# Moving one half of k^T v across the partitions by transfers on GpSimd's queue instead of matmuls and copies, for four of eight batches

## The chip, the cores and the metric

The kernel runs on one core of one Trainium2 chip. Its time is the time on the device in microseconds (us). Beside the time of a run, the profile gives a span, which is the time from the first to the last instruction of one profiled execution.

## The reference

Two blocks follow each other. The first is a linear attention without a softmax over 8 batches, 8 heads, 576 rows and 64 columns a head, with a norm of each row:

```python
kv = np.einsum('bhsd,bhse->bhde', k, v)
out = np.einsum('bhsd,bhde->bhse', q, kv)
rms = np.sqrt(np.mean(out * out, axis=-1, keepdims=True) + 1e-06)
return (out / rms * g_norm)
```

Its result, as 4608 tokens of 512 columns, enters a mixture of 8 experts: a token with `x @ w_skip > 0` goes to the expert with the largest of `x @ w_gate`, whose two layers (512 to 1024, relu, 1024 to 512) are weighted by the softmax and added to the token; the others stay as they are. All is in fp32.

## The kernel before, in words

**Stages.** The attention stage comes first. The experts follow, each with its weights loaded, its tokens gathered by indirect transfers, two layers, and the results scattered. Order on every engine is written out by hand (`tc.manual_schedule()`): what a function emits first runs first on its engine, and each engine and each DMA queue takes its instructions in that order.

**Units.** The attention's products with q are cut into 36 units. Batches 0 to 3 are units 0 to 15, four each; units 16 and 17 take the ninth row of each group of nine for these four batches together; batches 4 to 7 are units 18 to 33, and units 34 and 35 are again the ninth rows. The loop `for n in range(NU + 2)` emits a unit a turn: `turn(n + 1)` transposes q on PE (L460) and copies it on ACT (L463), `root(n - 1)` takes a root on ACT (L525), then come the jobs listed as "early", `values(n)` (PE L496, or L504 for the ninth rows, then ACT's squares L510), `squares` (DVE L518) and `norm(n - 1)` (DVE L532 and L537), then the jobs listed as "pe". In the batch's first two units `values` also transposes the ninth row (`turn_8`, PE L479 and ACT L482). `finish` and `scale` give GpSimd its work: small sums for the logits (L554, L558, L562), the product with g_norm (L567), and now and then a store of 256 KB on its own queue (L598). The other stores and all loads are on SP's queue.

**k^T v.** For each batch `state` builds k^T v in PSUM with 72 small matmuls (L379, 64x64 tiles of the array, shown as 144 instructions), cut into portions of so many of the 18 row groups, one portion a unit; `portions` gives for each batch the first unit and the sizes. After the last portion ACT copies the sums to `kvd` (L386), two diagonal blocks, called `own(b, w)`: w = 0 lies in partitions 0 to 63, w = 1 in 64 to 127. `state_t` (PE L393, ACT L396) turns them, `state_m` (PE L402, ACT L405) multiplies them with the gate's weights and adds 9 columns at each end.

**The exchange.** `values` needs each block in both halves of the partitions. `state_s` does this with two matmuls against an identity (PE L411, 64 partitions, 292 columns) into the other half of PSUM and two copies on ACT (L415) into `kvds[b % KVD]`. It is listed one unit after `state_m`. The first `values` that reads batch b's block is its first unit (18, 22, 26 and 30 for batches 4 to 7).

**What hangs on the units.** Streams of routing work (`choose`, `rank`, `number`, `rank_experts`, `early`) begin after units 12 and 22 and emit two or four DVE instructions a unit. At unit 30 `early` places PE's L869 after `values(30)`; its result gives the rows of the first gather (L863, on GpSimd's queue), whose tokens PE turns in L801. The first expert's first layer (L814) follows the attention stage.

Of the kernel before, what the change touches and what calls it, by code (L numbers as in the profile page):

```python
# [17 lines left out]
def kernel(  # L18
# [43 lines left out]
    nc = tc.nc  # L62
# [18 lines left out]
    KVD = 5  # L81
# [46 lines left out]
    def load_kv(b):  # L128
        if b < B:
            for name, to in (("k", kts), ("v", vts)):  # L130
                to[b] = kv_pool.tile([P, 4, C, D], FP32, tag=name, name=name)
            for u in range(2):
                for src, t in ((k, kts[b]), (v, vts[b])):
                    load_part(t, src, b, u)

    def load_q(b):
        if b < B:
            qts[b] = load(q_pool, "q", q, b)
# [65 lines left out]
    kvds = []  # L204
# [89 lines left out]
    for lo, m, _ in runs:  # L294
# [26 lines left out]
        out=srow[:, :].rearrange("p (r c) -> p r c", c=CK),  # L321
# [33 lines left out]
    def own(b, w):  # L355

        return kvds[b % KVD][w * 64:(w + 1) * 64, :, w, w, :]
# [13 lines left out]
    def state(b, some):  # L371

        kt, vt = kts[b], vts[b]
        for i in some:
            u, c = divmod(i, C)
            for w in range(2):
                for a in range(2):
                    r = slice(a * 64, (a + 1) * 64)
                    nc.tensor.matmul(  # L379
                        out=sum_ps[w * 64:(w + 1) * 64, a, u, :],  # L380
                        lhsT=kt[r, 2 * u + w, c, :], rhs=vt[r, 2 * u + w, c, :],
                        start=(c == 0), stop=(c == C - 1), skip_group_check=True)
        if some.stop < 2 * C:
            return
        for w in range(2):
            nc.scalar.copy(out=own(b, w)[:, :, G:G + 2 * D].rearrange("p u (a d) -> p a u d", a=2),  # L386
                           in_=sum_ps[w * 64:(w + 1) * 64, :, :, :])

    def state_t(b):
        for u in range(2):  # L390
            for w in range(2):
                r = slice(w * 64, (w + 1) * 64)
                nc.tensor.matmul(out=kvT_ps[:, u, r], lhsT=kvds[b % KVD][:, u, w, w, G:G + 2 * D],  # L393
                                 rhs=ident[:, r], start=True, stop=True)
        kvT = att_pool.tile([P, 2, P], FP32, tag="kvT", name="kvT", bufs=1)
        nc.scalar.copy(out=kvT[:, :, :], in_=kvT_ps)  # L396
        kvTs[b] = kvT

    def state_m(b):
        kvT = kvTs.pop(b)  # L400
        for u in range(2):
            nc.tensor.matmul(out=lg_ps[:, u, :, :, :], lhsT=kvT[:, u, :], rhs=gw_b[:, u, :, :, :],  # L402
                             start=True, stop=True)
        for w in range(2):
            nc.scalar.copy(out=ends_of(own(b, w)), in_=lg_ps[w * 64:(w + 1) * 64, :, :, w, :])  # L405

    def state_s(b):

        for w in range(2):
            r, o = slice(w * 64, (w + 1) * 64), slice((1 - w) * 64, (2 - w) * 64)  # L410
            nc.tensor.matmul(out=sw_ps[o, :], lhsT=ident[r, r], rhs=own(b, w), start=True, stop=True,  # L411
                             skip_group_check=True)
        for w in range(2):
            o = slice((1 - w) * 64, (2 - w) * 64)
            nc.scalar.copy(out=kvds[b % KVD][o, :, w, 1 - w, :],  # L415
                           in_=sw_ps[o, :].rearrange("p (u k) -> p u k", u=2))


    units = []
    nq = 0  # L420
# [21 lines left out]
    def at(step, part, job):  # L442
        todo.setdefault((step, part), []).append(job)
# [448 lines left out]
    for b in range(KNOWN // S // 4 * 4, KNOWN // S):  # L892
        nc.gpsimd.dma_start(
            out=out[b * S:(b + 1) * S, :].rearrange("(p c) d -> p c d", c=C)[:, C - 1, :],
            in_=zero)

    starts = {}
    for n, (_, b, i, _) in enumerate(units):
        if i is not None:
# [8 lines left out]
    turn(1)  # L908
    state_s(0)

    portions = {1: (1, (10, 8)), 2: (4, (6, 6, 6)), 3: (7, (5, 6, 7)), 4: (11, (3, 4, 4, 4, 3)),
                5: (16, (3, 2, 6, 7)), 6: (20, (4, 4, 5, 5)), 7: (24, (4, 4, 5, 5))}
    over = 0
    for b, n in starts.items():
        if b:
            step, counts = portions[b]
            i = 0
            for count in counts:
                at(step, "pe", lambda b=b, some=range(i, i + count): state(b, some))
                i += count  # L920
                step += 1
            assert i == 2 * C and step < n and step - len(counts) > over - 1
            at(step, "early", lambda b=b: state_t(b))
            at(step, "pe", lambda b=b: state_m(b))
            at(step + 1, "early" if step + 1 == n else "pe", lambda b=b: state_s(b))
            over = step
        at(over, "end", lambda b=b: load_kv(b + 3))

        at(n + 2, "end", lambda b=b: load_q(b + 2))
# [61 lines left out]
    with tc.tile_pool(name="wpool_b", bufs=1, reuse_waits="tile") as wpool_b, \  # L991
# [524 lines left out]
        with tc.If(n_rounds > 1):  # L1516
            with tc.For_i(1, n_rounds, 1):
# [8 lines left out]
                    out=left[:, :].rearrange("p (r c) -> p r c", c=CK),  # L1526
# [39 lines left out]
```

## Time and profile before

| What | Value |
|---|---|
| Time, median of 3 runs | 377.03 us (375.7 to 379.55) |
| The profiled execution's own time | 378.6 us |
| Its span | 376.7 us |
| Mean granted TensorE clock | 0.992 |
| PE busy | 362.9 us, 96% of the span |
| PE weight loads busy | 314.8 us, 84% |
| DVE, ACT, GpSimd busy | 244.3, 142.9, 122.7 us |
| Data moved | 81.70 MB, mean 217 GB/s |
| PE L411, one instruction | 405 ns, 32 of them |
| ACT L415, one copy | 397 ns, 16 of them |

A row of a timeline gives the start, the time to the end of the last instruction, the engine, the line, the operation with the tile written and the tiles read, and how many instructions it merges; in brackets, how long the engine sat idle before and what ended that. PE's rows overlap, because matmuls are pipelined: the time that a row holds PE is read from its start to the start of the next. DMA share is the mean busy share of the core's 16 DMA engines.

### The profile page before, as it was taken

The numbers are of one execution on the slowest core, as the hardware profiler recorded it, in microseconds if no ns is written. First come the engines' busy times: TensorE is split into PE (matmuls) and PEld (weight loads), VectorE is DVE, ScalarE is ACT, GpSimd is POOL, SyncE is SP. The second block draws the span as 40 slices with busy tenths as digits, with TensorE's granted clock in tenths as the row PEclk, the third lists the DMA queues.
The fourth block names the chain that finished last, engine by engine and source line by source line (L and its number), as shares of the span: only waits on it lengthen the run. The fifth ranks groups of instructions, "written<-read, shape, count | busy, mean of one in ns | idle before, by whom it ended". The sixth has DMA issues, their size and how long they took to land.

```text
span 376.7 us, 9624 instructions
## 1 busy us (share of the span) xinstructions
PE 362.9 (96%) x3848; PEld 314.8 (84%) x3848; DVE 244.3 (65%) x626; ACT 142.9 (38%) x383; POOL 122.7 (33%) x195
## 2 busy tenths in 40 slices
PE   8899999999988999999999999999999999999994
PEld 4687897898977948779979987988998998998983
DVE  3355367767787763566766675876876776878831
ACT  2466576666773212214402430430440430431420
POOL 7035467655668435323013302202302302102003
PEclk9999999999998999999999999999999999999998
DMA  8999999996487718967427362671762762700001
GB/s 289 395 391 391 401 405 396 405 384 206 132 302 213 232 39 281 392 237 252 168 98 222 114 225 76 239 244 46 284 197 72 274 209 80 269 3 28 30 1 53
DMA packets 32039, 81.70 MB, mean 217 GB/s; under 512 B 2474, under 2 KB 2482, under 8 KB 31988
## 3 DMA queue, kind: packets, MB, share of 16 engines
q1 hardware_dynamic: 28176, 69.47, 52.0%
q0 software_dynamic: 3792, 11.53, 9.2%
q8 instruction: 32, 0.52, 0.6%
q14 instruction: 19, 0.16, 0.1%
q10 hardware_dynamic: 20, 0.02, 0.0%
HBM read 66.80 MB, written 14.48 MB: 216 GB/s over the span
## 4 chain that ended last, share of the span: by engine, by line
PE 82%; issue 6%; DMA 3%; ACT 3%; DVE 3%; POOL 2%; SPq 0%; POOLq 0%; DVEq 0%; ACTq 0%
PE bank L1192 44%; PE bank L1124 9%; PE o_ps L496 6%; PE sum_ps L379 4%; PE bank L1112 4%; PE q_ps L460 3%; PE g_ps L393 2%; DMA v<-in_v_dram 2%; PE bank L1093 2%; PE q_ps L814 1%; DMA xg<-out_dram,src 1%; DVE rs L518 1%; DVE xl L537 1%; ACT sq L510 1%; PE g_ps L411 1%
## 5 line engine op out<-in xcount | busy, mean ns | idle before, releaser
L1202 ACT COPY p<-bank 128x128 f32<-128x128 f32 (+6 forms) x70 | 20.8, 297 | 99.2 <-PE bank L1192 88.5
L1192 PE MATMUL bank<-xt,w 128*128 128x128 f32 (+5 forms) x336 | 55.4, 288 | 0.0
L567 POOL TENSOR_TENSOR xb<-xl,g_b 128x512 f32<-128x512 f32 x36 | 43.5, 1211 | 32.5 <-DVE rs L532 30.6
L1323 POOL DMA_INDIRECT out_dram<-xg,rows x14 | 14.4, 1027 | 120.8 <-DVE xg L1320 117.6
L1192 PEld LDWEIGHTS bank<-xt,w 128*128 128x128 f32 x336 | 47.0, 190 | 1.9 <-DVE bank L1196 1.4
L1196 DVE TENSOR_TENSOR bank<-bank,p 128x128 f32<-128x128 f32 (+6 forms) x70 | 23.6, 337 | 30.2 <-PE bank L1192 29.1
L496 PE MATMUL o_ps<-kvd,qT 128*128 128x146 f32 x240 | 35.8, 290 | 1.0 <-ACT kvd L415 0.7
L1192 PE MATMUL bank<-xs,s 128*128 128x128 f32 (+5 forms) x224 | 36.7, 289 | 0.0
L518 DVE TENSOR_REDUCE rs<-sq 128x8 f32<-128x512 f32 x36 | 24.6, 682 | 15.3 <-ACT sq L510 15.1
L496 PEld LDWEIGHTS o_ps<-kvd,qT 128*128 128x128 f32 x240 | 31.6, 188 | 2.0 <-ACT kvd L415 1.5
L1124 PE MATMUL bank<-w,ht 128*32 128x128 f32 (+2 forms) x436 | 33.2, 318 | 0.0
L1192 PEld LDWEIGHTS bank<-xs,s 128*128 128x128 f32 x224 | 31.1, 190 | 1.0 <-ACT p L1202 0.8
L537 DVE TENSOR_TENSOR xl<-o_ps,rs 128x584 f32<-128x584 f32 x34 | 26.1, 767 | 4.5 <-DVE rs L532 0.5
L1124 PEld LDWEIGHTS bank<-w,ht 128*32 128x32 f32 (+2 forms) x436 | 19.3, 120 | 11.6 <-issue 8.3
L1192 PE MATMUL bank<-t,ht 128*128 128x256 f32 x112 | 27.0, 384 | 0.0
L1192 PE MATMUL bank<-w,ht 128*128 128x256 f32 x112 | 26.5, 380 | 0.0
L510 ACT ACTIVATE sq<-o_ps 128x512 f32<-128x512 f32 x34 | 20.3, 597 | 15.0 <-PE o_ps L496 14.4
L379 PE MATMUL sum_ps<-v,k 64*64 64x64 f32 x1152 | 24.7, 223 | 0.8 <-issue 0.6
L1192 PE MATMUL bank<-t,hs 128*128 128x256 f32 x112 | 25.3, 379 | 0.0
L379 PEld LDWEIGHTS sum_ps<-v,k 64*64 64x64 f32 x1152 | 20.9, 134 | 4.7 <-issue 1.7
L1084 POOL DMA_INDIRECT xg<-out_dram,src x14 | 13.8, 985 | 33.3 <-DMA out_dram<-xg,rows 17.3
L1192 PEld LDWEIGHTS bank<-t,ht 128*128 128x128 f32 x112 | 20.8, 190 | 3.9 <-issue 1.2
(217 smaller groups left out, 671.0 us busy)
## 6 DMA issues: line engine op xcount, KB each, us to landing
w<-in_moe_w_dram SPq DMA_DIRECT2D x16, 2048.0 KB, 10.0
k<-in_k_dram SPq DMA_DIRECT2D x16, 576.0 KB, 9.1
v<-in_v_dram SPq DMA_DIRECT2D x16, 576.0 KB, 11.0
q<-in_q_dram SPq DMA_DIRECT2D x16, 576.0 KB, 10.5
out_dram<-xb SPq DMA_DIRECT2D x29, 256.0 KB, 8.0
out_dram<-xb POOLq DMA_DIRECT2D x7, 256.0 KB, 6.4
xg<-out_dram,src POOLq DMA_INDIRECT x16, 3.5
out_dram<-xg,rows POOLq DMA_INDIRECT x16, 6.0
```

What stands on the lines that cost most here:

```text
L379: nc.tensor.matmul(out=sum_ps[w * 64:(w + 1) * 64, a, u, :], lhsT=kt[r, 2 * u + w, c, :], rhs=vt[r, 2 * u + w, c, :], start=(c == 0), stop ...
L496: nc.tensor.matmul(out=ps[:, w, 0:2 * PK].rearrange("p (r k) -> p r k", r=2)[:, :, cols], lhsT=qT[:, w, a, :], rhs=kvds[b % KVD][:, u, w, ...
L510: nc.scalar.activation(out=sq[:, :, :, :], in_=heads(ps, G, G + 2 * D), func=ACT.Square)
L518: nc.vector.tensor_reduce(out=rs[:, :, :], in_=sq[:, :, :, :].rearrange("p x y (a d) -> p x (y a) d", a=2), axis=AX.X, op=ALU.add)
L537: nc.vector.tensor_tensor(out=xl[:, :, :, :].rearrange("p x y (a k) -> p x (y a) k", a=2), in0=ps[:, :, 0:2 * PK].rearrange("p x (h k) -> ...
L567: late.append((lambda: nc.gpsimd.tensor_tensor(out=xb[:, :, 4 * u * D:(4 * u + 4) * D].rearrange("p r (w x) -> p r w x", w=2), in0=xl[:, : ...
L1112: nc.tensor.matmul(out=hps[:, cols], lhsT=w_sb[r][0][:, dc, f * P:(f + 1) * P], rhs=xt[:, dc, cols], start=(dc == 0), stop=(dc == DC - 1))
L1124: nc.tensor.matmul(out=yps[q * m:(q + 1) * m, 0:n], lhsT=ht(f)[:, off:off + m], rhs=w_sb[r][1][:, f, q * n:(q + 1) * n], start=(f == 0), s ...
L1192: nc.tensor.matmul(out=out, lhsT=lhsT(i), rhs=rhs(i), start=start and i == 0, stop=i == k - 1, skip_group_check=True)
L1196: nc.vector.tensor_tensor(out=to, in0=x, in1=y, op=ALU.add)
L1202: nc.scalar.copy(out=t, in_=x)
L1323: ins = nc.gpsimd.indirect_dma_start(out=cut_rows(m)[:, :], out_offset=bass.IndirectOffsetOnAxis(ap=rows[:, col:col + 1], axis=0), in_=x, ...
```

## The change

For batches 4 to 7 `state_x` takes the place of `state_s`. It issues two transfers on GpSimd's queue, from each diagonal block to the other half of the partitions in the same tile. They are listed in the same unit as `state_t` and `state_m`, behind `state_m`. The portions of these four batches become one fewer and larger, so that `state_t`, `state_m` and the transfers come one unit earlier (units 15, 19, 23 and 27, where before `state_t` stood in 16, 20, 24 and 28 and `state_s` in 17, 21, 25 and 29). Batches 0 to 3 stay as they are. The lines of the new kernel behind this point are 6 to 9 higher.

```diff
+    def state_x(b):
+
+        for w in range(2):
+            o = slice((1 - w) * 64, (2 - w) * 64)
+            nc.gpsimd.dma_start(out=kvds[b % KVD][o, :, w, 1 - w, :], in_=own(b, w))
...
-    portions = {1: (1, (10, 8)), 2: (4, (6, 6, 6)), 3: (7, (5, 6, 7)), 4: (11, (3, 4, 4, 4, 3)),
-                5: (16, (3, 2, 6, 7)), 6: (20, (4, 4, 5, 5)), 7: (24, (4, 4, 5, 5))}
+    portions = {1: (1, (10, 8)), 2: (4, (6, 6, 6)), 3: (7, (5, 6, 7)), 4: (11, (4, 5, 5, 4)),
+                5: (16, (5, 6, 7)), 6: (20, (6, 6, 6)), 7: (24, (6, 6, 6))}
...
-            at(step + 1, "early" if step + 1 == n else "pe", lambda b=b: state_s(b))
+            if b < 4:
+                at(step + 1, "early" if step + 1 == n else "pe", lambda b=b: state_s(b))
+            else:
+                at(step, "pe", lambda b=b: state_x(b))
```

## The prediction

> **What bounds the kernel now.** I read the page's chain that ended last first, then the chain in order of time over the attention stage, then the timelines of PE and of GpSimd there, then the busy time by stretches with the DMA share, and last the line that already sends plain transfers from GpSimd's queue.
>
> The page says which engine sets the end:
>
> ```profile
> PE 82%; issue 6%; DMA 3%; ACT 3%; DVE 3%; POOL 2%; SPq 0%; POOLq 0%; DVEq 0%; ACTq 0%
> PE bank L1192 44%; PE bank L1124 9%; PE o_ps L496 6%; PE sum_ps L379 4%; PE bank L1112 4%; PE q_ps L460 3%; PE g_ps L393 2%; DMA v<-in_v_dram 2%; PE bank L1093 2%; PE q_ps L814 1%; DMA xg<-out_dram,src 1%; DVE rs L518 1%; DVE xl L537 1%; ACT sq L510 1%; PE g_ps L411 1%
> ```
>
> PE carries it, and L411, the swap that the change removes, is 1% of the span. The change touches only the stage before about 107 us, so I ask what ends that stage. PE's timeline near its end (start us, us, engine, line, operation):
>
> ```profile
> 100.73 1.22 PE L496 MATMUL o_ps<-kvd,qT 128*128 128x146 f32 x8
> 101.78 0.53 PE L402 MATMUL g_ps<-gw_b,kvT 128*128 128x36 f32 x4
> 102.15 0.64 PE L460 MATMUL q_ps<-ident,q 128*128 128x128 f32 x4
> 102.62 1.17 PE L496 MATMUL o_ps<-kvd,qT 128*128 128x146 f32 x8
> 103.71 0.71 PE L411 MATMUL g_ps<-kvd,ident 64*64 64x292 f32 x4
> ...
> 105.06 1.18 PE L496 MATMUL sum_ps<-kvd,qT 128*128 128x146 f32 x8
> 106.29 0.69 PE L869 MATMUL g_ps<-bv,oha_k 128*128 128x4 bf16 x22
> ...
> 111.94 0.63 PE L801 MATMUL q_ps<-ident,xg 128*128 128x128 f32 x4 [1.10 <-DMA xg<-out_dram,src]
> ```
>
> Each L496 row is one unit's `values`; 100.73, 102.62 and 105.06 are units 28, 29 and 30, and unit 30 is the first that reads batch 7's swapped half. L869 stands behind it on PE, its rows start the gather that L801 waits 1.10 us for, and all to 117 us hangs on that. So what counts is when unit 30's product and L869 run: lateness there passes to the end one to one.
>
> GpSimd's timeline where it sends half a block of rows as a plain transfer, and the answer on that line:
>
> ```profile
> 99.74 0.58 POOL L598 DMA_DIRECT2D out_dram<-xb  x1 [0.29 <-POOL xb L567]
> ```
>
> ```profile
> DMA to landing us min/median/max: 4.5/6.4/7.4
> ```
>
> And the stretches (length, busy us of PE, PEld, DVE, ACT, POOL, then PEclk, DMA share, GB/s):
>
> ```profile
> 70.00:80.00 10.00, 10.00 (x195) 9.22 (x194) 7.58 (x18) 6.61 (x19) 6.25 (x13) 1.00 1.04 402
> 80.00:90.00 10.00, 9.79 (x175) 8.66 (x177) 6.86 (x17) 7.19 (x18) 6.54 (x11) 1.00 0.71 235
> 90.00:98.00 8.00, 7.96 (x160) 7.29 (x161) 6.19 (x22) 5.16 (x14) 3.90 (x9) 1.00 0.45 167
> 98.00:106.00 8.00, 8.00 (x97) 6.91 (x96) 6.74 (x18) 6.16 (x16) 5.44 (x9) 1.00 0.83 264
> ...
> 112.00:118.00 6.00, 4.19 (x83) 3.50 (x84) 4.70 (x10) 3.21 (x8) 5.44 (x11) 1.00 0.60 146
> 118.00:122.00 4.00, 4.00 (x16) 4.00 (x16) 2.95 (x7) 0.49 (x2) 3.33 (x9) 0.57 0.95 285
> ```
>
> PE has no free time from 70 to 106 us, so instructions taken off it there are worth their time. But the DMA engines are full to about 85 us and again at 98 to 106, and a plain transfer of GpSimd's needs 4.5 to 7.4 us there. The last two rows show the clock: after a stretch with PE 70% busy it fell to 0.57.
>
> **What the Trainium skill says.** "DMA: Bandwidth & Descriptors", "Anatomy of one DMA — SWDGE (gpsimd) path", prices a transfer at 2.0 us plus its bytes over 436e3 per us: for one half of the exchange (64 x 2 x 146 x 4 = 74,752 bytes) an estimate of 2.2 us. The trace differs: 256 KB stores would take 2.6, and took 6.4. Its "Queues, rings and completion order" says that an engine takes turns between queues a packet at a time; in the trace's packet records the stores' first packet starts 3.9 to 4.4 us after the issue in all six stores before 100 us, and 2.4 us in the one of 113.93, where less was in flight. So sharing delays the start more than the data. "TensorEngine Tiling (Array Packing)", "Key Properties", says that a change of tiling mode drains TensorE. The trace agrees in size: L379 rows of 32, 40, 48 and 56 instructions hold PE for 0.63, 0.74, 0.86 and 0.97 us to the next row, so 0.0143 each and 0.17 fixed. "TensorE: Matmul & The Clock Gate", "What's actually happening", has the clock fall to half after a slack window of 3.4 us; here it was at half from 118.2 to 121.6 us.
>
> **The change part by part.** Removed from PE: the swap for batches 4 to 7. Beside L379 (units 17, 21, 25) it costs 0.42, 0.47, 0.48: 80.22 to 81.32 is 1.10 with 32 products of 0.63. Alone (unit 29) it costs 0.64. Sum 2.0. Four portions fewer save 4 x 0.17 = 0.7. From ACT: eight L415 copies of 0.40, 3.2 us; ACT is about 65 to 75% busy, so that only frees its queue.
>
> Moved: each batch's L393, L402 and copies run one unit earlier, and the later portions are larger. L393 still waits for the L386 copies (0.58 us in unit 16 before, 0.2 in unit 24); with nothing turned ahead of unit 15 I expect 0.6 there. k and v of batches 5 to 7 were issued by 45, 56 and 69 us and first used at 64, 76 and 88, so one unit earlier costs nothing; that cover is about 10 us. Batch 7's load is issued a unit sooner into full engines, also covered.
>
> Added: eight issues on GpSimd's in-order queue, two each in units 15, 19, 23, 27, 0.6 us each (L598's 0.58). The first waits for ACT's L405 copies, the last step of the batch; behind it stand `lp`, the next `xb`, and the logits. GpSimd is 60 to 65% busy and idles 1.3 to 2.2 us before many `xb`, so it has caught up before `choose` asks at units 22 and 34: nothing. In units 23 and 27 L598 goes out just ahead on the same queue. SP's queue is not passed, but its loads and stores are what fills the engines.
>
> The unknown is L, issue to landing of a half: from 2.9 (fastest gather of L863) to 7.4. I take 5.0: first packet at 3.9, then about 1 for two packets per engine and the slowest engine, where a store has four. The second half lands 0.6 later.
>
> Now each batch's cycle, end of one first `values` to the next. To the issue: last portion 0.9, turn 0.62, L393 1.2, turn of the ninth row 0.22, `values` 1.1, then ACT 0.60 + 0.37 + 0.37: about 5.5. Then L + 0.6, and the second half of `values` 0.55: 11.65 at L = 5.0. PE's own work in the cycle, without that wait:
>
> - Batch 4, from PE's rows: unit 14 starts at 59.4 (59.03, and 24 more products ahead of it). Its product 1.2, 32 products 0.63, the wait 0.6, L393 1.2, unit 15's product 1.1, L402 0.5: 64.65, and L405 is done at 65.25. From 64.65 unit 16 0.67, 40 products 0.74, ranks 0.70, turn 0.57, unit 17 0.56, 48 products 0.86, turns 0.88: unit 18 could start at 69.6 (70.07 before). Issue at 65.3, landings 70.3 and 70.9: it ends at 71.5 against 71.17. **+0.3**.
> - Batch 5: PE alone 11.5, transfer 11.65; before 11.96 (71.17 to 83.13). **-0.3**.
> - Batch 6: PE alone 12.2 with the ranks' 0.7; transfer 11.7 to 12.2; before 12.59. **-0.4**.
> - Batch 7: PE and DVE 10.3, before 10.5. The transfer stands behind the store of 99.74, whose last packet started 7.05 us after it, at 106.8, while expert 0's first weights load; so L is nearer 5.7 and the cycle 12.35. **+1.85**.
>
> Sum **+1.5 us**. The profiled execution took 378.6 with a span of 376.7, so 378.2 in that span. The median is 377.03, 1.6 under that execution, and I add the sum to it: **378.5**. After L869 nothing changes.
>
> **Rivals.** *Hidden transfers* (not slower): if L is under 3.8 every half lands before its product. Then batches 4 to 6 gain 0.3, 0.45 and 0.4, and L869 is held by DVE's `bv`, which follows unit 28 by 5.56 us (100.73 to 106.29): about -1.1, so 375.9. For it: the skill's price, and gathers that land in 2.9 to 3.8. Against it: every store before 100 us. It decides where batch 7's L falls below 3.8.
>
> *Late in every batch*: above L = 5.3 each cycle is the transfer's own and a microsecond of L costs a microsecond four times. At L = 6.4, the stores' median: +1.7, +1.1, +0.5 and +2.5, so +5.8: 382.8; at 5.9 about +3.8. For it: saturated engines; against it: a half has under a third of a store's bytes.
>
> *The clock*: the wait at unit 30 leaves PE idle about 2 us in 103 to 107. If a window there counts as slack, unit 30 and L869 run at half clock, 1.5 us more: 380.0.
>
> *No effect*: PE's saving and the waits cancel: 377.0.
>
> **How the numbers follow.** Likeliest 0.42 (own range 377.3 to 379.8), hidden 0.20, late 0.20, clock 0.12, no effect 0.06. Leaving a tenth at each end gives 375.6 to 381.8. One per cent is 3.8 us, about what a measurement here can tell from none (the three runs spread over 3.85). Slower by more: three quarters of late, a third of clock, a little of the likeliest: 0.21. Faster by more needs over three times the hidden gain: 0.02. Within: 0.77.
>
> **What would show it.** L411 16 times instead of 32 and L415 8 instead of 16; the new transfers at about 65, 77, 89 and 101 us with landings near 5; a wait of PE's L496 row for kvd of about 2 us before unit 30 and under 0.6 at the other three; L869 near 107.8. A wait below 0.5 at unit 30 means that hidden is right; over 1 us in all four, late. If `lp` or `lg` ended DVE's waits longer than before, my zero for GpSimd was wrong.

## The result, and the profile after

The changed kernel takes 387.68 us (median of 6 runs, 385.26 to 389.42), the kernel before beside it 377.83 us (6 runs, 375.7 to 379.55). The ratio is 1.0257, with a 95% interval of 1.0226 to 1.0288: slower by 2.6%, where 378.5 us and "no change" were forecast. The profiled execution took 389.31 us with a span of 387.4, 10.7 us more than the span before.

The page's chain that ended last (the work that set the end of the program, followed back), by engine and by line, has a new name near its head:

```profile
PE 76%; issue 8%; DMA 5%; POOL 4%; ACT 3%; DVE 3%; ACTq 0%; POOLq 0%; DVEq 0%
PE bank L1201 43%; PE bank L1133 9%; PE o_ps L502 6%; PE bank L1121 4%; DMA kvd<-kvd 3%; PE sum_ps L379 3%; PE q_ps L466 2%; POOL xb L573 2%; PE bank L1102 2%; PE g_ps L393 1%; DMA w<-in_g_norm_dram 1%; PE q_ps L170 1%; DVE xl L543 1%; PE q_ps L820 1%; DVE rs L524 1%
```

PE's share fell from 82% to 76%, the swap L411 is gone from the list, and `DMA kvd<-kvd`, the exchange, holds 3% of the span. PE's timeline shows where (start us, us, engine, line, operation; in brackets the idle time before it and what ended it). L502 is the former L496, L875 the former L869, L820 the former L814:

```profile
72.30 2.31 PE L502 MATMUL o_ps<-kvd,qT 128*128 128x146 f32 x8 [2.04 <-DMA kvd<-kvd]
...
86.78 1.34 PE L502 MATMUL o_ps<-kvd,qT 128*128 128x146 f32 x8 [1.37 <-DMA kvd<-kvd]
...
100.61 1.27 PE L502 MATMUL o_ps<-kvd,qT 128*128 128x146 f32 x8 [1.90 <-DMA kvd<-kvd]
...
114.66 2.31 PE L502 MATMUL sum_ps<-kvd,qT 128*128 128x146 f32 x8 [3.65 <-DMA kvd<-kvd]
116.77 0.77 PE L875 MATMUL g_ps<-bv,oha_k 128*128 128x4 bf16 x22
...
129.71 2.87 PE L820 MATMUL q_ps<-xt_first,w 128*128 128x192 f32 x16 [0.44 <-ACT xt_first L836]
```

The first unit of every exchanged batch (18, 22, 26 and 30) waits for its block: 2.04 + 1.37 + 1.90 + 3.65 = 8.96 us. Two of the four rows last 2.31 us in place of some 1.2: PE runs at half clock there. L875 comes 10.5 us later than L869 did (106.29). The experts' first layer, L820, comes 12.5 later than L814 did, but takes 2.87 us for 4.55, because now it meets the full clock. That leaves 10.8, the difference of the spans within 0.1. The same two products in the kernel before, the first of unit 18 with no wait ahead of it:

```profile
70.07 1.17 PE L496 MATMUL o_ps<-kvd,qT 128*128 128x146 f32 x8
...
117.23 4.55 PE L814 MATMUL q_ps<-xt_first,w 128*128 128x192 f32 x16 [0.44 <-ACT xt_first L830]
```

GpSimd's timeline has the issues, and the answer on L423 the time to the landing:

```profile
66.01 1.25 POOL L423 DMA_DIRECT2D kvd<-kvd  x2 [1.36 <-ACT kvd L405]
80.58 1.23 POOL L423 DMA_DIRECT2D kvd<-kvd  x2 [1.39 <-ACT kvd L405]
93.97 1.19 POOL L423 DMA_DIRECT2D kvd<-kvd  x2 [0.78 <-ACT kvd L405]
107.27 1.19 POOL L423 DMA_DIRECT2D kvd<-kvd  x2 [0.50 <-ACT kvd L405]
```

```profile
DMA to landing us min/median/max: 6.1/6.5/7.2
```

The answer covers five of the eight halves; the other three have no landing on record. From the first issue of a batch to PE's start there are 6.29, 6.20, 6.64 and 7.39 us. And the stretches around two of the waits (length, busy us of PE, PEld, DVE, ACT, POOL, then PEclk, DMA share, GB/s):

```profile
70.00:75.00 5.00, 2.96 (x26) 2.42 (x28) 1.72 (x5) 1.01 (x3) 3.32 (x7) 0.72 1.04 375
...
110.00:115.00 5.00, 1.34 (x10) 1.11 (x10) 2.73 (x8) 1.37 (x3) 2.27 (x5) 0.81 0.98 336
115.00:120.00 5.00, 4.75 (x40) 4.57 (x40) 2.22 (x8) 1.59 (x4) 1.51 (x2) 0.50 0.15 57
120.00:125.00 5.00, 5.00 (x30) 4.99 (x29) 2.61 (x5) 2.50 (x6) 3.92 (x7) 0.66 0.28 79
```

While PE waits, the DMA engines are full (share 0.98 to 1.04), and what follows the wait runs at a clock of 0.5 to 0.7. In the trace's clock records the half clock lies at 72.17 to 75.58 and 113.13 to 123.37.

Two questions follow: is 6 to 7 us what such a transfer takes, or what it takes behind other traffic; and is there a place in the program from which it is hidden?

### The profile page after: what moved, and what is told of

The parts are those of the page before. It is cut to its first block, busy times and chain, and to the rows that moved or that the text cites. A ratio compares the mean times of both kernels' runs of the same rounds, so it can differ in the third digit from the quotient of the medians.

```text
span 387.4 us, 9601 instructions
## 1 busy us (share of the span) xinstructions
PE 364.9 (94%) x3832; PEld 317.1 (82%) x3832; DVE 245.7 (63%) x626; ACT 140.2 (36%) x375; POOL 129.5 (33%) x203
## 4 chain that ended last, share of the span: by engine, by line
PE 76%; issue 8%; DMA 5%; POOL 4%; ACT 3%; DVE 3%; ACTq 0%; POOLq 0%; DVEq 0%
PE bank L1201 43%; PE bank L1133 9%; PE o_ps L502 6%; PE bank L1121 4%; DMA kvd<-kvd 3%; PE sum_ps L379 3%; PE q_ps L466 2%; POOL xb L573 2%; PE bank L1102 2%; PE g_ps L393 1%; DMA w<-in_g_norm_dram 1%; PE q_ps L170 1%; DVE xl L543 1%; PE q_ps L820 1%; DVE rs L524 1%
## 5 line engine op out<-in xcount | busy, mean ns | idle before, releaser
L573 POOL TENSOR_TENSOR xb<-xl,g_b 128x512 f32<-128x512 f32 x36 | 44.4, 1234 | 29.3 <-DVE rs L538 27.4
L502 PE MATMUL o_ps<-kvd,qT 128*128 128x146 f32 x240 | 38.6, 305 | 6.8 <-DMA kvd<-kvd 5.3
L1205 DVE TENSOR_TENSOR bank<-bank,p 128x128 f32<-128x128 f32 (+6 forms) x70 | 23.6, 338 | 30.3 <-PE bank L1201 28.1
L502 PEld LDWEIGHTS o_ps<-kvd,qT 128*128 128x128 f32 x240 | 34.1, 201 | 8.8 <-DMA kvd<-kvd 6.1
L516 ACT ACTIVATE sq<-o_ps 128x512 f32<-128x512 f32 x34 | 20.3, 596 | 23.8 <-PE o_ps L502 23.6
L1093 POOL DMA_INDIRECT xg<-out_dram,src x14 | 14.8, 1056 | 33.3 <-DMA out_dram<-xg,rows 17.8
L379 PE MATMUL sum_ps<-v,k 64*64 64x64 f32 x1152 | 24.2, 230 | 0.5 <-issue 0.5
L379 PEld LDWEIGHTS sum_ps<-v,k 64*64 64x64 f32 x1152 | 20.9, 143 | 4.2 <-issue 2.2
## 6 DMA issues: line engine op xcount, KB each, us to landing
v<-in_v_dram SPq DMA_DIRECT2D x16, 576.0 KB, 10.7
```

The lines of the kernel that those rows point to most:

```text
L379: nc.tensor.matmul(out=sum_ps[w * 64:(w + 1) * 64, a, u, :], lhsT=kt[r, 2 * u + w, c, :], rhs=vt[r, 2 * u + w, c, :], start=(c == 0), stop ...
L502: nc.tensor.matmul(out=ps[:, w, 0:2 * PK].rearrange("p (r k) -> p r k", r=2)[:, :, cols], lhsT=qT[:, w, a, :], rhs=kvds[b % KVD][:, u, w, ...
L516: nc.scalar.activation(out=sq[:, :, :, :], in_=heads(ps, G, G + 2 * D), func=ACT.Square)
L573: late.append((lambda: nc.gpsimd.tensor_tensor(out=xb[:, :, 4 * u * D:(4 * u + 4) * D].rearrange("p r (w x) -> p r w x", w=2), in0=xl[:, : ...
L1093: nc.gpsimd.indirect_dma_start(out=x_of(xg, off, m), out_offset=None, in_=cut_rows(m)[:, :], in_offset=bass.IndirectOffsetOnAxis(ap=idx[:, ...
L1205: nc.vector.tensor_tensor(out=to, in0=x, in1=y, op=ALU.add)
```

## The experiments

**1. The parts of the change.** First the new portions with the swap by matmuls, which is still one unit after `state_m` and so one unit earlier than before:

```diff
-            if b < 4:
-                at(step + 1, "early" if step + 1 == n else "pe", lambda b=b: state_s(b))
-            else:
-                at(step, "pe", lambda b=b: state_x(b))
+            at(step + 1, "early" if step + 1 == n else "pe", lambda b=b: state_s(b))
```

> The new portions for batches 4 to 7, with the exchange by PE and ACT (state_s) one unit after state_m as before. If the transfers' latency is the whole loss: PE drops four portions of 0.17 us, so about 0.7 us less, and no loss: 376.5 to 378.0. If the larger portions or the earlier turn of k^T v (waits of L393 for L386) carry part of the loss: 379 or more, up to 388 if they carry all of it.

379.67 us (10 runs), ratio 1.0037 (1.0012 to 1.0062): a small part of the loss. The ranks' transposes now wait for the copies L415 (0.85 and 0.51 us). To take that out as well, the swap went back to the units where it was before (`step + 2` for batches 4 to 7), so that only the portions and `state_t`, `state_m` differ:

> The new portions with the exchange by state_s in its old units (17, 21, 25, 29) for all four batches, so that it no longer stands ahead of the ranks of units 16 and 24 as in the run with the portions alone. If the 1.4 us lost there were those waits of the ranks for the bank: 376.5 to 378. If the larger portions cost by themselves: 379 or more.

378.64 us (22 runs), ratio 1.0027 (1.0009 to 1.0044), between the two cases that were expected. The larger portions save nothing. PE's timeline shows what stands against the 0.7 us forecast for four portions fewer, three gaps before k^T v's products that nothing in the profile explains ("issue"):

```profile
66.94 0.33 PE L379 MATMUL sum_ps<-v,k 64*64 64x64 f32 x2 [0.22 <-issue]
...
73.03 0.93 PE L379 MATMUL sum_ps<-v,k 64*64 64x64 f32 x48 [0.55 <-issue]
...
86.22 0.34 PE L379 MATMUL sum_ps<-v,k 64*64 64x64 f32 x6 [0.79 <-issue]
```

They sum to 1.6 us; the last section comes back to them. So the portions cost about 1 us and, by difference, the transfers the other 9.

Then the transfers for batch 7 alone, the others with the swap in its old units:

```diff
-            if b < 4:
-                at(step + 1, "early" if step + 1 == n else "pe", lambda b=b: state_s(b))
+            if b < 7:
+                at(step + 1 if b < 4 else step + 2, "early" if step + 1 == n else "pe", lambda b=b: state_s(b))
```

> The new portions, with the exchange by transfers for batch 7 alone; batches 4 to 6 by state_s two units after state_t, where it stood before. If each wait counts for itself: 3.7 us of wait before unit 30, about 2.5 us more for the half clock behind it, 0 to 1 us less for the saved swap: 382 to 384. If batch 7 was late only because the earlier batches' waits had pushed things together: 378 to 380.

383.31 us, ratio 1.0161 (1.0128 to 1.0193), as expected if each wait counts for itself. One exchange alone brings back the largest wait, with half clock from 107.16 to 113.99 behind it (101.91 is unit 29, 107.28 unit 30):

```profile
101.91 1.27 PE L502 MATMUL o_ps<-kvd,qT 128*128 128x146 f32 x8 [0.79 <-DVE xl L543]
...
107.28 2.31 PE L502 MATMUL sum_ps<-kvd,qT 128*128 128x146 f32 x8 [3.45 <-DMA kvd<-kvd]
...
109.38 0.77 PE L875 MATMUL g_ps<-bv,oha_k 128*128 128x4 bf16 x22
```

```profile
DMA to landing us min/median/max: 6.9/7.0/7.1
```

**2. The clock.** Idle matmuls, whose results nobody reads, fill the four waits (8, 6, 8 and 14 of them, ahead of units 18, 22, 26 and 30):

```diff
+    FILL = {18: 8, 22: 6, 26: 8, 30: 14}
...
+        if n in FILL:
+            fill_ps = ps_q.tile([P, 512], FP32, tag="q", name="q_ps")
+            for _ in range(FILL[n]):
+                nc.tensor.matmul(out=fill_ps[:, :], lhsT=ones[:, :],
+                                 rhs=ones[:, :].unsqueeze(1).to_broadcast([P, 4, P]), start=True, stop=True)
```

> The change, with idle matmuls of 128x512 bf16 (0.25 us each) on PE in the four waits: 8, 6, 8 and 14 of them ahead of units 18, 22, 26 and 30. They compute nothing that is used. If the clock's fall in the waits costs about 3 us (half clock at 72 to 76 and 113 to 123 us): the clock stays at 1.0 there and the time falls to 384 to 386. If the clock is a side effect without cost: 387 to 389.

385.75 us, ratio 1.0197 (1.016 to 1.0233), with a mean clock of 0.996 in the profiled execution, where the changed kernel had 0.976 (0.976 to 0.990 in its six runs). No half clock is left before 130 us, and the time falls by about 2 us of the 10; the waits themselves are the larger part. The fill costs something itself: ahead of units 26 and 30 it runs past the landing of the first half (100.32 and 114.23), and the units start at 101.27 and 115.37. So 2 us is the least that the clock costs.

**3. Is it GpSimd's queue?** The same transfers from ACT's queue:

```diff
-            nc.gpsimd.dma_start(out=kvds[b % KVD][o, :, w, 1 - w, :], in_=own(b, w))
+            nc.scalar.dma_start(out=kvds[b % KVD][o, :, w, 1 - w, :], in_=own(b, w))
```

> The eight exchange transfers issued on ACT's queue in place of GpSimd's, nothing else changed. If the 3.9 to 4.8 us from issue to the first packet belong to sharing the engines with SP's loads, whatever the queue: landing stays at 6 to 7 us and the time at 386 to 389. If they belong to GpSimd's queue: landing near 3 us, no waits of over 0.5 us before units 18, 22, 26, 30, and about 377. If GpSimd's blocked queue (sums and xb behind the waiting transfer) were the cause, the time would fall to about 378 even with late landings.

387.73 us, ratio 1.0283 (1.0221 to 1.0345). The answer on the line and two of the waits (summed us, times, longest):

```profile
DMA to landing us min/median/max: 5.3/7.2/7.9
```

```profile
PE q_ps L466 <- ACT qT L469: 2.8, 3, 1.4
...
PE sum_ps L502 <- DMA kvd<-kvd: 1.4, 1, 1.4
PE o_ps L502 <- DMA kvd<-kvd: 1.2, 2, 0.9
```

The landing (on record for three of the eight halves) is as long from the other queue, and the time stays with GpSimd's queue free of it; so that queue is not the cause. The waits for `kvd` shrink to 2.6 us, at least in part because PE is late for another reason: ACT's issues take up to 1.5 us each, and PE waits 2.8 us for ACT's copies of q.

**4. Issuing earlier.** Three times the portions were moved so that the issue comes earlier. First about two units, by larger portions:

```diff
-    portions = {1: (1, (10, 8)), 2: (4, (6, 6, 6)), 3: (7, (5, 6, 7)), 4: (11, (4, 5, 5, 4)),
-                5: (16, (5, 6, 7)), 6: (20, (6, 6, 6)), 7: (24, (6, 6, 6))}
+    portions = {1: (1, (10, 8)), 2: (4, (6, 6, 6)), 3: (7, (5, 6, 7)), 4: (11, (9, 9)),
+                5: (15, (6, 6, 6)), 6: (18, (6, 6, 6)), 7: (21, (6, 6, 6))}
```

> The transfers as in the change, but with portions (9, 9) for batch 4 and (6, 6, 6) for 5, 6, 7 begun earlier, so that the exchange is issued in units 13, 18, 21 and 24 (before: 15, 19, 23, 27) for use in 18, 22, 26 and 30. If latency alone is the loss, every landing is 2 to 7 us ahead of its use, the waits and the slow clock vanish and PE keeps its 2.7 us: 375 to 377. If GpSimd's queue or the transfers' share of the engines is the loss: 382 or more.

388.51 us, ratio 1.0274 (1.0237 to 1.0311): no wait for `kvd` is left, and no time is won. The time is in the case "382 or more", but its two reasons are not what the trace shows. PE's timeline has new gaps in the products that were moved:

```profile
58.28 0.45 PE L379 MATMUL sum_ps<-v,k 64*64 64x64 f32 x11 [1.51 <-issue]
...
74.22 1.13 PE L379 MATMUL sum_ps<-v,k 64*64 64x64 f32 x31 [3.29 <-issue]
```

The second one brings half clock from 72.76 to 79.59, and unit 18 starts at 78.21, in the kernel before at 70.07. From there to unit 30 it takes 33.75 us against 34.99 before, with no wait for a transfer in it. But 104 products of L379, one L393 and three swaps fewer lie in that stretch, an estimated 4 us of PE's work (0.0143 us a product, 1.2 and 1.6 us, the prediction's own prices), of which only 1.2 come out as time: near its end PE waits for DVE's `xl` (0.95 us at 110.20). The landings of this run are telling (six of eight are on record):

```profile
DMA to landing us min/median/max: 2.3/3.5/7.4
```

The slow one belongs to the exchange of 63.49, in full traffic; those issued from 81.59 to 100.69 landed in 2.3 to 4.2.

Next the portions as even as possible, so that no large one stands alone:

```diff
+    portions = {1: (1, (10, 8)), 2: (4, (6, 6, 6)), 3: (7, (5, 6, 7)), 4: (10, (4, 5, 5, 4)),
+                5: (14, (4, 4, 5, 5)), 6: (18, (6, 6, 6)), 7: (21, (4, 4, 5, 5))}
```

> The transfers as in the change, but batches 4 to 7 begin their portions earlier in pieces of 4 to 6 row groups: (4, 5, 5, 4) from unit 10, (4, 4, 5, 5) from 14, (6, 6, 6) from 18, (4, 4, 5, 5) from 21. The exchange is issued in units 14, 18, 21, 25 for use in 18, 22, 26, 30. If landing time against lead is the whole loss and the stalls of the run with two units earlier came from squeezing the products: no wait of over 0.5 us for kvd, no gap of PE with no cause shown over 0.7 us, and 375.5 to 378. If the exchange by transfers has a cost of its own, over 380.

384.23 us, ratio 1.0179 (1.0141 to 1.0217). Again no wait for `kvd`; a gap of 2.53 us ahead of L379 at 71.73 with half clock to 77.3, and unit 18 at 74.55. Less early work in the full stretch loses less, but it still loses: the gap that was not to come over 0.7 us is there, and the time is over 380.

Last, batches 4 and 5 as in the kernel before, and only 6 and 7 by transfers, in portions of 9, issued after the full stretch (the diff is against the kernel before):

```diff
-                5: (16, (3, 2, 6, 7)), 6: (20, (4, 4, 5, 5)), 7: (24, (4, 4, 5, 5))}
+                5: (16, (3, 2, 6, 7)), 6: (20, (9, 9)), 7: (23, (9, 9))}
...
-            at(step + 1, "early" if step + 1 == n else "pe", lambda b=b: state_s(b))
+            if b < 6:
+                at(step + 1, "early" if step + 1 == n else "pe", lambda b=b: state_s(b))
+            else:
+                at(step, "pe", lambda b=b: state_x(b))
```

> Batches 4 and 5 keep the portions and the swap by matmul of the kernel before; batches 6 and 7 go by the transfers, in portions of 9 and 9 products, with their issue four and five units ahead of their first use, behind the stretch in which the loads fill the engines (it ends near 85 us). If the loss is the landing under full load and the fetch of instructions at the smaller, earlier portions, both are avoided: no wait for kvd, and two swaps less save about 1.1 us and up to 0.7 for fewer portions: 375.5 to 378. If the transfers carry a cost of their own that an early issue does not hide (a slower gather, the engines taken from the weights), over 380.

386.65 us, ratio 1.0206 (1.0176 to 1.0236), above the 375.5 to 378 of one theory and in the other's "over 380". No wait for `kvd` is in it, but PE and GpSimd show this:

```profile
85.18 0.66 PE L393 MATMUL g_ps<-ident,kvd 128*128 128x64 f32 x5 [1.25 <-issue]
...
93.11 1.58 PE L502 MATMUL o_ps<-kvd,qT 128*128 128x146 f32 x8 [2.18 <-DVE xl L543]
...
108.91 1.27 PE L502 MATMUL o_ps<-kvd,qT 128*128 128x146 f32 x8 [1.25 <-DVE xl L543]
```

```profile
88.81 1.25 POOL L423 DMA_DIRECT2D kvd<-kvd  x2 [2.95 <-ACT kvd L405]
```

The gap delays L393 and with it L405; GpSimd's queue stands still for 2.95 us before the issue, the logits' sums behind it come late, DVE waits 2.59 us for them, PE waits 2.18 for DVE, and the clock is at half from 93.92 to 97.34. Unit 30 starts at 110.67 (105.06 before). From 105 to 110 us DVE is busy for 4.51 of 5 us: the products that were taken out of these units shorten nothing, since DVE holds the pace there. So the second theory's outcome came, but by other ways than it named: the early issue has a price in PE's order and in GpSimd's. How much of the loss each of these makes up was not tested.

**5. What stands ahead of the transfer.** In the changed kernel SP's queue issues loads of q (1.18 MB) at 79.90 and 93.02 and the first expert's weights (2 MB) at 102.62, each 0.7 to 4.7 us before an exchange. With the q loads of batches 6 and 7 two units later:

```diff
-        at(n + 2, "end", lambda b=b: load_q(b + 2))
+        at(n + 2 if b < 4 else n + 4, "end", lambda b=b: load_q(b + 2))
```

> The change, with the loads of q for batches 6 and 7 put two units later on SP's queue, behind the exchange of batches 5 and 6 rather than just ahead of it. If the landing of 6 to 7 us is the queueing behind such a load: the exchange of batches 5 and 6 lands in 2.5 to 4 us and the waits before units 22 and 26 (1.37 and 1.90 us) vanish, those before 18 and 30 stay: 384 to 386. If the landing is a property of the transfer: 386 to 389.

389.03 us, ratio 1.0313 (1.0278 to 1.0349). The exchange of batch 6 (issue 91.85) now had its last data packet start 2.35 us after the issue, and unit 26 no longer waits. The exchange of batch 5 (issue 78.41) did not follow what was expected: it landed after 5.6 and 6.8 us, counted from the first issue, with a load of q issued 0.5 us behind it, and unit 22 still waits 0.84 and 0.38 us. And q itself came late:

```profile
PE q_ps L466 <- DMA q<-in_q_dram: 9.5, 2, 9.3
...
PE o_ps L502 <- DMA kvd<-kvd: 3.3, 3, 2.1
```

So the reason is right for batch 6, is not shown for batch 5, and the edit pays with 9.3 us elsewhere.

A cleaner test leaves the loads of q, k and v for batches 4 to 7 out altogether (earlier batches' tiles are read again), in the changed kernel and in the kernel before:

> The changed kernel with the loads of q, k and v for batches 4 to 7 left out (earlier batches' tiles are used again, so the routing and what follows differ; only the attention stage is compared). If the landing is long because the loads fill the engines: landings of 2.3 to 3.5 us, no wait for kvd above 0.5 us, and the last unit's end within 1 us of the same stage of the kernel before without those loads. If the landing is a property of the transfer: 6 to 7 us again, and waits of about 9 us in sum.

> The kernel before with the same loads left out, as the measure for the other: its attention stage should end within 2 us of the 106 us that it takes with the loads, as its profile shows no wait for a load in batches 4 to 7.

Only the attention stage is compared, in one execution of each; the routing then sends the tokens otherwise, and the whole runs (1064.21 and 1060.0 us) say nothing. Here `values` is L506 in the changed kernel and L500 in the kernel before. The changed kernel's waits for `kvd`, with unit 29 between them:

```profile
70.58 1.27 PE L506 MATMUL o_ps<-kvd,qT 128*128 128x146 f32 x8 [0.50 <-DMA kvd<-kvd]
...
102.30 1.27 PE L506 MATMUL o_ps<-kvd,qT 128*128 128x146 f32 x8 [0.79 <-DVE xl L547]
...
107.73 2.32 PE L506 MATMUL sum_ps<-kvd,qT 128*128 128x146 f32 x8 [3.50 <-DMA kvd<-kvd]
```

Units 18 and 29 of the kernel before without the loads:

```profile
70.88 1.17 PE L500 MATMUL o_ps<-kvd,qT 128*128 128x146 f32 x8
...
103.42 1.17 PE L500 MATMUL o_ps<-kvd,qT 128*128 128x146 f32 x8
```

Of four waits two are gone and one is down from 2.04 to 0.50 us. The landings were not as short as expected in every batch: the last data packet starts 3.9, 3.8 and 2.4 us after the first issue of batches 4, 5 and 6, where it was 5.9, 5.7 and 6.2 with the loads. From unit 18 to unit 29 it takes 31.72 us (70.58 to 102.30), against 32.54 in the kernel before without the loads: there the change gains 0.8 us, with 48 products and two swaps fewer in the stretch. The fourth wait stays, against what was expected; only loads of q, k and v had been left out, and the weights still go out ahead of it, on SP's queue:

```profile
98.01 0.40 SPq L340 DMA_DIRECT2D w<-in_moe_w_dram  x1
```

The exchange is issued at 100.49 behind these 2 MB, and its first packet starts 4.84 us later. The kernel before took 34.99 us from unit 18 to unit 30 with the loads and 34.99 without them: to it they are free there.

The last run tests that fourth wait. It is the kernel with batch 7 alone by transfers, but the weights' load waits for the exchange to land:

```diff
-            load_weights(0, wpool_a, later=True)
+            at(29, "end", lambda: load_weights(0, wpool_a, sent[-1], later=True))
...
-            nc.gpsimd.dma_start(out=kvds[b % KVD][o, :, w, 1 - w, :], in_=own(b, w))
+            sent.append(nc.gpsimd.dma_start(out=kvds[b % KVD][o, :, w, 1 - w, :], in_=own(b, w)))
```

> As with transfers for batch 7 only, and the first expert's first weights (2 MB) loaded only when the exchange has landed, so that they do not stand ahead of it. If the wait of 3.45 us ahead of unit 30 and the half clock after it come from that load: no wait for kvd above 1 us, no half clock near 107, and a time of 376.5 to 379, the later weights still being there near 116, where they are first used; a gather that now shares the engines with them could cost up to 2 us more. If the landing is a matter of the transfer itself: a wait above 2.5 us again and 382 to 385.

```profile
DMA to landing us min/median/max: 2.6/2.9/3.1
```

```profile
104.22 1.27 PE L504 MATMUL o_ps<-kvd,qT 128*128 128x146 f32 x8 [0.79 <-DVE xl L545]
105.98 1.17 PE L504 MATMUL sum_ps<-kvd,qT 128*128 128x146 f32 x8
...
108.06 0.69 PE L877 MATMUL g_ps<-bv,oha_k 128*128 128x4 bf16 x22 [0.92 <-DVE bv L858]
...
116.57 1.08 PE L809 MATMUL q_ps<-ident,xg 128*128 128x128 f32 x4 [4.02 <-DMA xg<-out_dram,src]
```

The landing falls from 6.9 to 7.1 us with batch 7 alone to 2.6 to 3.1, the wait is gone, and from unit 29 to L877 it is 3.84 us where it was 7.47 (101.91 to 109.38). (Unit 29 itself starts 2.3 us later here; that arises before the exchange, as unit 18 is already 1.5 us later.) That part of the expectation holds. The time does not: 383.74 us, ratio 1.0147 (1.0122 to 1.0171), because the weights, issued at 105.67, now stand ahead of the first gather (issue 109.68), which lands after 6.76 us and before took 3.83. PE waits 4.02 us for it, 1.10 in the kernel before, and the clock is at half from 115.40 to 125.64. The price of that collision was put at up to 2 us and is nearer 4: from L877 to the experts' first layer it takes 15.20 us (108.06 to 123.26), 10.94 before. No version tried beats the kernel before.

The traces taken together say what kind of traffic counts. A full DMA share alone does not: over the first 2 us after the issue it is 0.99 in the last run and 0.92 at the issue of 91.85 with q later, where the first half lands in 3.1 and 2.7 us, and 0.81 to 1.04 at the four exchanges of the change, whose halves take 6.1 to 7.2 us. But each exchange on GpSimd's queue whose first half takes over 6 us has a load of k, v, q or weights issued in some 5 us ahead of it, and each that takes under 4 us has none there, only stores of 256 KB or nothing.

## Why the prediction was wrong, point by point

**The step that failed** is L, "from 2.9 (fastest gather of L863) to 7.4. I take 5.0: first packet at 3.9, then about 1 for two packets per engine and the slowest engine ... The second half lands 0.6 later." The range held; the value did not. In the packet records the first packet of the four exchanges starts 3.9, 4.1, 4.15 and 4.85 us after the first issue, as taken from the stores. But the last packet of both halves starts 5.7 to 7.0 us after it, so the data take about 2 us, not 1: the packets last 0.2 to 0.5 us each, but their starts are spread over 1.7 to 2.1 us. PE starts on the first half, 0.04 and 0.05 us after its landing in batches 5 and 6, and the second half lands 0.6 and 0.5 us later, as forecast. So L, taken to PE's start, is 6.3, 6.2 and 6.6 us where 5.0 was taken, and 7.4 where 5.7 was. That puts 1.3, 1.2, 1.65 and 1.7 us on PE, 5.8 of the 9.0 by which L875 (116.77) missed the forecast 107.8.

**The second part** is the clock. It was a rival alone, at 1.5 us for unit 30. It came on top of the late landings, and twice: 3.4 us of half clock at unit 18, worth 1.7, and about 0.9 from unit 30 to L875. These leave 0.6 of the 9.0, about what the first issue was later than forecast (66.01 for 65.3). After L875 the half clock costs about 2 us more to L820, and 1.7 come back in L820 itself: 2.9 us in all by this reckoning, where the filled waits, whose fill runs past two landings, gave 2. The Trainium skill, "TensorE: Matmul & The Clock Gate", "What's actually happening", gives windows of 3.4 us; the half-clock stretches here are 3.41 and 10.24 us, one and three of them. A wait of 2 us was enough to lose one at unit 18, though not at unit 26 (1.90). What differs is where the wait falls: in each of the 14 traces all changes of the clock lie whole multiples of 3.41 us apart. On that grid in the changed kernel's trace, PE's matmuls leave 57% idle of the window that ends at 72.17 and 62% of the one that ends at 113.13, but boundaries at 85.82 and 99.48 cut the waits of units 22 and 26 in two, and no window there is idle for more than about a third. The limit is not sharp: 51% passed without a fall in the run with two units earlier, while 37% brought one with the even portions and 33% one on ACT's queue. So whether a wait of 2 us loses the clock is in part luck, but the clock belonged into the case of late landings, not beside it.

**The rival that was right** is *late in every batch*, held at 0.20 with 382.8 us at L = 6.4. Waits over 1 us in all four units were its sign, and there they are. What was said against it, that "a half has under a third of a store's bytes", misled: 3.9 to 4.85 us are spent before the first byte. Full engines, the argument for it, were in the stretches that the prediction showed (1.04 and 0.83), though it is the loads issued just ahead that tell late landings from early ones. And its own sum lacked the clock. The case of most chance and this one were told apart by 1.4 us of one unknown; the range should have reached to the stores' median plus the clock, some 385.

**Four portions fewer, 0.7 us saved**: wrong. The same portions with the swap in its old place measured 1.0 us slower, not faster. The page that the prediction names for the drain states no size, so the fixed 0.17 us of a row agrees with nothing there.

**"One unit earlier costs nothing", as the loads have 10 us of cover**: right for k and v, no wait for them appears. But the loads were not the only thing the portions needed in time, as the gaps show. The terms of its "about 5.5" from a batch's first product to the issue add to 5.4; 5.9 and 5.4 were measured for batches 6 and 7, so this did not matter.

**Right**: L411 16 times and L415 8; issues of 0.6 us each; DVE's wait for the logits no longer than before, so GpSimd's order cost nothing here (in the run with two late batches it did). The largest wait before unit 30. Without the loads, units 18 to 29 gain 0.8 us, near the 0.7 that was forecast for batches 5 and 6, in one execution.

**What stays open.** That a load ahead makes the landing long is shown by taking it away, for batch 7 with the weights (2.6 to 3.1 for 6.9 to 7.1 us) and for batch 6 with q. For batch 4, where loads of k, v and q stand close together, only the run without any of them speaks. How the engines share is not shown. The Trainium skill's "DMA: Bandwidth & Descriptors", "Queues, rings and completion order", says that an engine empties a whole packet of typically 9 to 17 descriptors before it turns to the next queue. If each 4,096-byte record of the trace, at 0.159 us, is one descriptor, a turn is an estimated 1.4 to 2.7 us, and the first packet's delay beyond the 1.2 to 2.4 us seen with no load in the 5 us ahead is 1.5 to 3.6: about one turn. If a record is a whole packet, a turn is 0.16 us and explains nothing. No run separates either from a backlog that is served first.

## What to carry to other kernels

Price a small transfer by what is issued ahead of it on any queue, not by its bytes: read the loads that go out in the 5 us before it rather than the DMA share alone, and take the slowest of like transfers, to the last engine. The swap by matmuls cost PE 0.4 to 0.6 us a batch and waited for no transfer; a transfer in its place must here be issued 7 to 8 us ahead where loads stand before it, and if what moves it ahead takes cover from other work, or if what is put behind it collides with the next transfer, that is part of its price. Add the clock as a risk to waits of about 2 us or more.

## What the runs showed of the hardware that was not expected

PE seems to wait for its own instructions. The gaps before L379 and L393 that end with "issue" have no data as their releaser. In the trace's packet records the queue named "instruction" moves packets of 16,384 bytes through the same DMA engines. In all 27 such gaps on PE before 130 us, in 14 traces, PE resumes 1.22 to 1.54 us after the end of one of these packets, of which a trace has 14 to 16 in that time: in the run with two units earlier, the packet of 71.76 to 72.83 and the start at 74.22. Of the gaps, 13 stand at 23.6 to 25.1 us, ahead of all that the change touches, in the kernel before too. Of the other 14, those with the portions of the change are 0.2 to 0.8 us long (its own trace has none), and those with denser ones 1.25 to 3.29. A reading that fits is that many short matmuls put together use up PE's instructions before the next packet comes, and that loads make that packet late. It rests on times that agree, not on a run with the fetches taken away.
